# Reordering the mixer of a gated-attention-and-mixer kernel: the low-rank update a chunk ahead, the last chunk's second product kept for the next batch boundary, GpSimd transfers in written order

## The chip, the cores and the metric

The kernel runs on one core of a Trainium2 chip. The metric is the device time of one execution, in microseconds (us). Before the change it is 1245.14 us, the median of three runs (1243.36 to 1246.68). In this text PE is the matrix engine (PEld its weight loads), DVE the vector engine, ACT the scalar engine, POOL is GpSimd, and SP is the engine that issues the transposing transfers and the stores.

## The reference, cut to what matters

```python
# 8 batches; u, v: (8, 3136, 256); z: (8, 3136, 64); all float32
scores = (1.0 / S) * np.matmul(z, z.transpose(0, 2, 1))
x = u * np.matmul(np.maximum(scores, 0.0) ** 2, v)          # gated attention
xt = x.transpose(0, 2, 1)                                   # then the mixer
h = xt @ U @ V                                              # U: (3136, 32), V: (32, 3136)
u2 = x + h.transpose(0, 2, 1)
out = u2 + np.maximum(u2 @ w_ch1, 0.0) @ w_ch2              # 256 -> 1024 -> 256
```

## The kernel before

Each batch has 25 tiles of 128 rows. Attention handles one tile per turn (25 matmuls of 256 columns, 2.73 us). The scores are symmetric, so the kernel computes half of them and gets the other half by transposing DMAs ("strip"). When a pair of tiles is done, DVE multiplies it by u into `x_bf`, and SP transposes it into `uT`. When all 25 tiles are done comes the batch boundary: the rank product `x^T U` (t1), then the mixer, in seven chunks of three or four tiles. For every chunk there is

- a **mix**: two matmuls give V^T t1 for the chunk, and DVE adds them into `uT` in place;
- four **up** steps: `uT` times w_ch1, and ACT applies the relu;
- a **down** step for each tile: relu times w_ch2 (with one matmul more for the tile's V^T t1), and a DVE output add when a tile or a pair of tiles is done.

```python
ps2_pool = ctx.enter_context(tc.tile_pool(name="ps2", bufs=2, space=bass.MemoryType.PSUM))
# mm() chains every matmul to the one before, so PE runs in the order written.

def mix_steps(b, c):
    ...                                   # two matmuls into a ps2 buffer, then:
    dst = uT[:, :, c0 : c0 + w]
    dve(nc.vector.tensor_tensor(out=dst, in0=ps[:, :, :w], in1=dst, op=ALU.add), wait=False)

def mixer_steps(b, cs):
    steps = mix_steps(b, cs[0]) + up_steps(b, cs[0])
    for n, c in enumerate(cs):
        nxt = cs[n + 1] if n + 1 < len(cs) else None
        up = mix_steps(b, nxt) + up_steps(b, nxt) if nxt is not None else []
        down = down_steps(b, c)
        k = 0
        for i, s in enumerate(up):
            steps.append(s)
            while k < (i + 1) * len(down) // len(up):
                steps.append(down[k]); k += 1
        steps.extend(down[k:])
    return steps

# in each batch: chunks 3 to 6 of the batch before are spread into attention ("late")
    late = mixer_steps(b - 1, list(range(EARLY, NC))) if b else []
    ...
# at the boundary (cut): scores of the next batch, rank product, casts of v, then
    _spread(nxt[0], []); _spread(rank_steps(b), [])
    ...                                   # cast_v(0), cast_v(1), load_v
    _spread(nxt[1], [])
    early = mixer_steps(b, list(range(EARLY)))      # chunks 0 to 2
    early[0]()                                      # mix of chunk 0
    for s in rest[:3]: s()                          # two score steps and a strip
    for k, s in enumerate(early[1:]): s(); ...      # further score steps in between
```

Scores, mixes and up steps all draw on `ps2`, which has two buffers. A buffer comes free when ACT (scores, up) or DVE (mix) has read it. From chunk 1 on, a mix stands directly ahead of the first up step of its chunk.

## Time and profile before

| | before |
|---|---|
| time, median | 1245.14 us |
| PE busy / weight loads | 91% / 69% |
| ACT / DVE busy | 44% / 40% |
| chain of waits | PE 83%; the DVE add into uT is next |
| holes of PE, per boundary-to-boundary period | 11.7 to 15.0 us |
| holes of PE in the last mixer | 12.9 us |

"Holes" are my own sum over the timeline of matmuls. A hole is the start-to-start time of two matmuls beyond what the first takes back to back (109 ns for 256 columns, 176 for 416, 216 for 512). A period runs from 5 us ahead of one rank product to 5 us ahead of the next. Measured so, holes are real lost slots, while a busy share of PE is not: the Trainium skill, "Perfetto Trace Analysis", section "Identifying the Most-Contended Engine", says that matmul occupancy misjudges a pipelined PE and that weight-load occupancy is better. Here the page shows 91% for matmuls and 69% for weight loads, and the gaps decide.

The page of the profile, before: busy time of each engine, and the clock that PE was granted in 40 slices (tenths).

```profile
PE 1130.8 (91%) x8808; PEld 852.6 (69%) x8808; DVE 491.6 (40%) x773; ACT 542.5 (44%) x627; POOL 109.7 (9%) x194
PEclk8699999999999999999999998999999999999999
```

The list of waits before, for weight loads (engine, what ended the wait: us in total, times, longest).

```profile
PEld L81 <- issue: 83.5, 178, 2.1
PEld L81 <- DVE uT L361: 58.0, 34, 2.8
PEld L81 <- DVE zT L155: 16.4, 1, 16.4
```

The chain of waits before, by line.

```profile
by line: DVE uT L361 3.8%; ACT relu L388 1.8%; issue 1.2%; DMA zP<-z_bf 1.2%; DMA strip<-A_102 0.8%; DVE v_bf L176 0.8%; DMA v_raw<-in_v_dram 0.6%; SPq L247 0.6%; DMA strip<-A_91 0.6%; DMA z_raw<-in_z_dram 0.5%; PE ps_348 L81 0.5%; PE ps_11
```

The timeline of PE before, at the second boundary (start, duration, what it computes, count; in brackets the idle time ahead of it and what ended it).

```profile
300.20 0.59 PE L81 MATMUL ps_2909<-V_bf,t_sb 128*128 128x512 bf16 x2 [0.60 <-ACT A_103 L237]
300.95 0.51 PE L81 MATMUL ps_2913<-zT 128*128 128x416 bf16 x2 [0.16 <-ACT A_103 L237]
302.11 0.51 PE L81 MATMUL ps_2918<-zT 128*128 128x416 bf16 x2 [0.64 <-DVE uT L361]
...
308.76 0.59 PE L81 MATMUL ps_2960<-V_bf,t_sb 128*128 128x512 bf16 x2 [0.40 <-ACT relu L388]
310.67 1.04 PE L81 MATMUL ps_2965<-uT,w_bf 128*128 128x512 bf16 x4 [1.32 <-DVE uT L361]
...
318.76 0.59 PE L81 MATMUL ps_3051<-V_bf,t_sb 128*128 128x512 bf16 x2
321.71 1.04 PE L81 MATMUL ps_3056<-uT,w_bf 128*128 128x512 bf16 x4 [2.35 <-DVE uT L361]
```

A mix is `V_bf,t_sb`, an up step is `uT,w_bf`. Each up step that directly follows its mix waits for the DVE add, for 1.3 and 2.35 us here. The add itself takes 1.22 us; the rest of the longer wait is a 0.95 us cast of v that DVE had in front.

### The profile page before, as it was taken

The page shows a single profiled execution, that of the slowest core. Times are in us where ns is not written, and L with a number is a line of the kernel's source. Part 1 is how long each engine was busy: PE and PEld are TensorE (multiplying, and loading weights), DVE is VectorE, ACT ScalarE, POOL GpSimd, SP SyncE. Part 2 cuts the span into 40 slices and gives each one's busy share as a digit, 9 for nine tenths or more (in the row PEclk, how much of TensorE's full clock was granted, in tenths as well). Part 3 has the DMA queues.
Part 4 walks back from the last instruction along what each step waited for, and adds up shares of the span by engine and source line. Part 5 has one row for each costly group of instructions (what it writes and reads, how often), then busy time and mean ns, then how long its engine had stood idle before and what let it go on. Part 6 is the DMA issues. An engine that isn't in the chain of part 4 may idle for free.

```text
span 1242.8 us, 21094 instructions
## 1 busy us (share of the span) xinstructions
PE 1130.8 (91%) x8808; PEld 852.6 (69%) x8808; DVE 491.6 (40%) x773; ACT 542.5 (44%) x627; POOL 109.7 (9%) x194
## 2 busy tenths in 40 slices
PE   2698989998899988999799998999889998899987
PEld 1277757785678856788477874778657885678845
DVE  4742534335343353424434253443543334332122
ACT  3441555436452464425645255542635346451043
POOL 2500100000000000010000000000000010000000
PEclk8699999999999999999999998999999999999999
DMA  8589846785558956598565865778746795267811
GB/s 196 121 179 180 172 135 158 155 175 149 147 129 179 167 125 145 128 190 150 134 153 136 190 149 126 156 157 170 164 123 140 168 175 135 77 135 153 159 36 71
DMA packets 418288, 182.93 MB, mean 147 GB/s; under 512 B 389728, under 2 KB 395664, under 8 KB 418192
## 3 DMA queue, kind: packets, MB, share of 16 engines
q1 hardware_dynamic: 402112, 121.71, 49.4%
q0 software_dynamic: 16080, 59.87, 17.5%
q8 instruction: 69, 1.13, 0.4%
q14 instruction: 27, 0.22, 0.1%
HBM read 61.91 MB, written 25.69 MB: 70 GB/s over the span
## 4 chain that ended last, share of the span: by engine, by line
PE 83%; DVE 7%; DMA 4%; ACT 4%; issue 1%; SPq 1%; DVEq 0%; ACTq 0%
DVE uT L361 4%; ACT relu L388 2%; DMA zP<-z_bf 1%; DMA strip<-A_102 1%; DVE v_bf L176 1%; DMA v_raw<-in_v_dram 1%; SPq L247 1%; DMA strip<-A_91 1%; DMA z_raw<-in_z_dram 1%; PE ps_348 L81 0%; PE ps_11941 L81 0%; PE ps_10502 L81 0%; PE ps_9471 L81 0%; PE ps_8957 L81 0%; PE ps_8637 L81 0%
## 5 line engine op out<-in xcount | busy, mean ns | idle before, releaser
L81 PEld LDWEIGHTS <-strip 128*128 128x128 bf16 x2400 | 235.6, 98 | 60.5 <-DMA strip<-A_102 6.1
L81 PEld LDWEIGHTS <-relu 128*128 128x128 bf16 x1600 | 160.2, 100 | 29.7 <-issue 2.5
L81 PEld LDWEIGHTS <-w_bf 128*128 128x128 bf16 x896 | 86.5, 100 | 121.7 <-DVE uT L361 58.0
L81 PEld LDWEIGHTS <-zT 128*128 128x128 bf16 x800 | 79.5, 100 | 82.7 <-issue 49.7
L265 POOL DMA_DIRECT2D u_sb<-in_u_dram x96 | 52.8, 550 | 707.4 <-DVE x_bf L292 701.1
L176 DVE CAST v_bf<-v_raw 128x1536 bf16<-128x1536 f32 x32 | 30.5, 953 | 3.0 <-DMA v_raw<-in_v_dram 3.0
L168 POOL DMA_DIRECT2D v_raw<-in_v_dram x32 | 18.8, 587 | 118.4 <-DVE zT L155 34.7
L81 PEld LDWEIGHTS <-V_bf 128*128 128x128 bf16 x200 | 20.0, 100 | 10.8 <-issue 2.4
L329 ACT CAST t_sb<-ps_11997 128x256 bf16<-128x256 f32 x1 | 0.4, 372 | 46.3 <-PE ps_11997 L81 46.3
L81 PEld LDWEIGHTS <-t_sb 128*128 128x128 bf16 x112 | 10.8, 97 | 13.8 <-issue 10.0
L238 DVE TENSOR_TENSOR A_106<-A_106 128x832 bf16<-128x832 bf16 x16 | 9.5, 591 | 25.5 <-ACT A_106 L237 25.5
L238 DVE TENSOR_TENSOR A_101<-A_101 128x832 bf16<-128x832 bf16 x16 | 12.2, 763 | 12.3 <-ACT A_101 L237 12.3
L238 DVE TENSOR_TENSOR A_110<-A_110 128x832 bf16<-128x832 bf16 x16 | 9.5, 593 | 18.2 <-ACT A_110 L237 18.2
L238 DVE TENSOR_TENSOR A_97<-A_97 128x832 bf16<-128x832 bf16 x16 | 10.4, 651 | 15.2 <-ACT A_97 L237 15.2
L238 DVE TENSOR_TENSOR A_108<-A_108 128x832 bf16<-128x832 bf16 x16 | 9.5, 592 | 17.0 <-ACT A_108 L237 17.0
L81 PE MATMUL ps_156<-zT 128*128 128x416 bf16 x2 | 0.9, 528 | 16.8 <-DVE zT L155 16.8
L238 DVE TENSOR_TENSOR A_109<-A_109 128x832 bf16<-128x832 bf16 x16 | 9.5, 593 | 16.1 <-ACT A_109 L237 16.1
L155 DVE COPY zT<-zP 64x1536 bf16<-64x1536 bf16 (+3 forms) x20 | 12.8, 642 | 7.6 <-DMA zP<-z_bf 7.1
L238 DVE TENSOR_TENSOR A_98<-A_98 128x832 bf16<-128x832 bf16 x16 | 9.4, 591 | 15.8 <-ACT A_98 L237 15.8
L238 DVE TENSOR_TENSOR A_112<-A_112 128x832 bf16<-128x832 bf16 x16 | 9.5, 592 | 15.5 <-ACT A_112 L237 15.5
L238 DVE TENSOR_TENSOR A_95<-A_95 128x832 bf16<-128x832 bf16 x16 | 9.4, 590 | 15.0 <-ACT A_95 L237 15.0
L238 DVE TENSOR_TENSOR A_111<-A_111 128x832 bf16<-128x832 bf16 x16 | 9.5, 593 | 14.6 <-ACT A_111 L237 14.6
(3457 smaller groups left out, 2984.6 us busy)
## 6 DMA issues: line engine op xcount, KB each, us to landing
v_raw<-in_v_dram POOLq DMA_DIRECT2D x32, 768.0 KB, 5.7
u_sb<-in_u_dram POOLq DMA_DIRECT2D x96, 256.0 KB, 3.7
out_dram<-o_sb SPq DMA_DIRECT2D x80, 256.0 KB, 2.3
z_raw<-in_z_dram POOLq DMA_DIRECT2D x7, 768.0 KB, 4.8
out_dram<-o_sb SPq DMA_DIRECT2D x32, 128.0 KB, 2.3
uT<-x_bf SPq DMA_TRANSPOSE x200, 3.5
v_tmp<-in_moe_V_dram POOLq DMA_DIRECT2D x8, 192.0 KB, 4.5
w_bf<-in_moe_w_ch_dram POOLq DMA_DIRECT2D x2, 512.0 KB, 8.9
```

The costliest lines, as they stand in the source:

```text
L81: ins = nc.tensor.matmul(**kw)
L155: nc.vector.tensor_copy(out=zT[:dqk, t0 + h : e : 2, :], in_=zP[h * dqk : (h + 1) * dqk, t0 // 2 : _ceil_div(e, 2), :],)
L168: nc.gpsimd.dma_start(out=v_raw, in_=rows(v[b])[:, k * n_v : (k + 1) * n_v, :])
L176: dve(nc.vector.tensor_copy(out=v_bf[:, k * n_v : (k + 1) * n_v, :], in_=v_raw))
L238: nc.vector.tensor_tensor(out=dst, in0=dst, in1=dst, op=ALU.mult)
L247: nc.sync.dma_start_transpose(out=strip, in_=slot(b, o)[:, P:])
L265: nc.gpsimd.dma_start(out=u_sb[:, :nq, :], in_=rows(u[b])[:, o : o + nq, :])
L329: nc.scalar.copy(out=t1_sb, in_=ps[:, :D])
L361: nc.vector.tensor_tensor(out=dst, in0=ps[:, :, :w], in1=dst, op=ALU.add),
L388: nc.scalar.activation(out=relu[:, hp : hp + 2, :w], in_=ps[:, :, :w], func=AF.Relu)
```

## The change

The change has three intents. Every mix is to be issued a chunk ahead of its up steps, so that the add is hidden. The last chunk's down steps are to be kept for the next boundary, where they fill the time of the score steps, of the t1 copy and of the first add. GpSimd's transfers are to be issued in written order instead of the scheduler's. Keeping the chunk needs four spare x tiles in odd batches, since the next batch's x would overwrite tiles 8 to 11. The steps are also merged more evenly, and the chunk sizes move from 4,4,4,4,3,3,3 to 4,4,4,3,3,3,4.

```diff
+    def pool_dma(**kw):                  # every GpSimd transfer chained to the one before
+        ins = nc.gpsimd.dma_start(**kw)
+        ...
-    x_bf = persist.tile([P, NT, D], BF16, name="x_bf")
+    x_bf = persist.tile([P, NT + SPARE, D], BF16, name="x_bf")      # SPARE = 4
...
+    def merge(*lists):                   # even interleaving by relative position
...
+    def mixer_steps(b, cs, down=()):
+        steps = []
         for n, c in enumerate(cs):
-            ...
+            steps += merge(up_steps(b, c), mix_steps(b, cs[n + 1]) if 0 < n < len(cs) - 1 else [], down)
+            down = down_steps(b, c)
...
-        late = mixer_steps(b - 1, list(range(EARLY, NC))) if b else []
+        if b:
+            cs = list(range(EARLY, NC))
+            late = mixer_steps(b - 1, cs, down_steps(b - 1, EARLY - 1))
+            left = down_steps(b - 1, NC - 1)
...
-            fill = fill + late[done:upto]
+            fill = merge(fill, late[done:upto])
             if more and i == NT - 8:             # as before, but now in this order on the queue
                 load_v(b + 1, 0)
                 load_v(b + 1, 1)
...
+        seq = merge(ahead[:2], left[:2]) + rank_steps(b) + merge(ahead[2:4], left[2:3])
+        seq += mix_steps(b, cs[0]) + left[3:] + ahead[4:5] + mix_steps(b, cs[1])
...
+            early = merge(early, vs, ahead[5:])
+            early += mix_steps(b, EARLY) + mix_steps(b, EARLY + 1)
```

More of the change, by code (lines that the diff above doesn't have):

```diff
@@ L89, in mm @@
         last[0] = ins.ins.name
+    last_pool = [None]
+    def pool_dma(**kw):
+        ins = nc.gpsimd.dma_start(**kw)
+        if last_pool[0] is not None:
+            tc.add_manual_dep(
+                ins.ins,
+                last_pool[0],
+                mybir.DependencyInfo(mybir.DependencyClass.NoSync, mybir.DependencyReason.DATA),
+                reason="pool order",
+            )
+        last_pool[0] = ins.ins.name
     last_dve = [None]
@@ L109 @@
     v_bf = persist.tile([P, NT, D], BF16, name="v_bf")
-    x_bf = persist.tile([P, NT, D], BF16, name="x_bf")
+    SPARE = 4
+    x_bf = persist.tile([P, NT + SPARE, D], BF16, name="x_bf")
     uT = persist.tile([P, ND, S], BF16, name="uT")
@@ L120, in col, with home @@
         return (t - FIRST) * P if t >= FIRST else S - FIRST * P + t * P
+    def home(b, t):
+        return NT + t - (FIRST - SPARE) if b % 2 and FIRST - SPARE <= t < FIRST else t
     def rows(ap):
@@ L126, with load_z @@
     z_tiles = {}
-    def load_z(b, parts, eng):
+    def load_z(b, parts, start):
         z_raw = stage.tile([P, NT, dqk], FP32, name="z_raw", tag="stage")
@@ L134, in load_z @@
         for t0 in range(0, NF, n):
-            eng.dma_start(out=z_raw[:, t0 : t0 + n, :], in_=rows(z[b])[:, t0 : t0 + n, :])
-        eng.dma_start(out=z_raw[:TAIL, NF, :], in_=z[b, NF * P :, :])
+            start(out=z_raw[:, t0 : t0 + n, :], in_=rows(z[b])[:, t0 : t0 + n, :])
+        start(out=z_raw[:TAIL, NF, :], in_=z[b, NF * P :, :])
         for t0 in range(0, NF, n):
@@ L167, in load_v @@
         if k < 4:
-            nc.gpsimd.dma_start(out=v_raw, in_=rows(v[b])[:, k * n_v : (k + 1) * n_v, :])
+            pool_dma(out=v_raw, in_=rows(v[b])[:, k * n_v : (k + 1) * n_v, :])
         else:
-            nc.gpsimd.dma_start(out=v_raw[:TAIL, 0, :], in_=v[b, NF * P :, :])
+            pool_dma(out=v_raw[:TAIL, 0, :], in_=v[b, NF * P :, :])
         v_tiles[k] = v_raw
@@ L180, in load_weights @@
     def load_weights():
-        nc.gpsimd.dma_start(out=w1_bf, in_=moe_w_ch1.rearrange("(t p) d -> p t d", p=P))
-        nc.gpsimd.dma_start(out=w2_bf, in_=moe_w_ch2.rearrange("(t p) d -> p t d", p=P))
-        nc.gpsimd.dma_start(out=U_bf[:, :NF, :], in_=rows(moe_U))
-        nc.gpsimd.dma_start(out=U_bf[:TAIL, NF, :], in_=moe_U[NF * P :, :])
+        pool_dma(out=w1_bf, in_=moe_w_ch1.rearrange("(t p) d -> p t d", p=P))
+        pool_dma(out=w2_bf, in_=moe_w_ch2.rearrange("(t p) d -> p t d", p=P))
+        pool_dma(out=U_bf[:, :NF, :], in_=rows(moe_U))
+        pool_dma(out=U_bf[:TAIL, NF, :], in_=moe_U[NF * P :, :])
         for p0 in range(0, P, P // 2):
@@ L188, in load_weights @@
             for g in range(G):
-                nc.gpsimd.dma_start(
+                pool_dma(
                     out=v_tmp[g * R : (g + 1) * R, :, :],
@@ L204, in load_weights @@
         for g in range(G):
-            nc.gpsimd.dma_start(
+            pool_dma(
                 out=v_tmp[g * R : (g + 1) * R, :TAIL], in_=moe_V[:, NF * P :]
@@ L264, in begin @@
                 if o < NF:
-                    nc.gpsimd.dma_start(out=u_sb[:, :nq, :], in_=rows(u[b])[:, o : o + nq, :])
+                    pool_dma(out=u_sb[:, :nq, :], in_=rows(u[b])[:, o : o + nq, :])
                 else:
-                    nc.gpsimd.dma_start(out=u_sb[:TAIL, 0, :], in_=u[b, NF * P :, :])
+                    pool_dma(out=u_sb[:TAIL, 0, :], in_=u[b, NF * P :, :])
                 acc[0] = (ps, u_sb)
@@ L292, in end @@
                     nc.vector.tensor_tensor(
-                        out=x_bf[:p, t0 : t0 + nq, :],
+                        out=x_bf[:p, home(b, t0) : home(b, t0) + nq, :],
                         in0=ps[:p, : nq * D].rearrange("p (t d) -> p t d", d=D),
@@ L301, in end @@
                     nc.sync.dma_start_transpose(
-                        out=uT[:, :, col(t) : col(t) + P], in_=x_bf[:, t, :]
+                        out=uT[:, :, col(t) : col(t) + P], in_=x_bf[:, home(b, t), :]
                     )
@@ L323, in run @@
                     lhsT=U_bf[:, t, :],
-                    rhs=x_bf[:, t, :],
+                    rhs=x_bf[:, home(b, t), :],
                     start=(t < G),
@@ L338 @@
     chunks = []
-    for i, n in ((0, 4), (4, 4), (8, 4), (12, 4), (16, 3), (19, 3), (22, 3)):
+    for i, n in ((0, 4), (4, 4), (8, 4), (12, 3), (15, 3), (18, 3), (21, 4)):
         ts = [turns(i + k) for k in range(n)]
@@ L437, in step @@
                         in0=ps[:p, : nk * D].rearrange("p (t d) -> p t d", d=D),
-                        in1=x_bf[:p, ta : ta + nk, :],
+                        in1=x_bf[:p, home(b, ta) : home(b, ta) + nk, :],
                         op=ALU.add,
@@ L456, in flat @@
         return [s for part in lists for s in part]
-    def mixer_steps(b, cs):
-        steps = mix_steps(b, cs[0]) + up_steps(b, cs[0])
+    def merge(*lists):
+        keyed = [
+            ((i + 0.5) / len(part), n, s)
+            for n, part in enumerate(lists)
+            for i, s in enumerate(part)
+        ]
+        return [s for _, _, s in sorted(keyed, key=lambda e: e[:2])]
+    def mixer_steps(b, cs, down=()):
+        steps = []
         for n, c in enumerate(cs):
-            nxt = cs[n + 1] if n + 1 < len(cs) else None
-            up = mix_steps(b, nxt) + up_steps(b, nxt) if nxt is not None else []
+            steps += merge(up_steps(b, c), mix_steps(b, cs[n + 1]) if 0 < n < len(cs) - 1 else [], down)
             down = down_steps(b, c)
-            k = 0
-            for i, s in enumerate(up):
-                steps.append(s)
-                while k < (i + 1) * len(down) // len(up):
-                    steps.append(down[k])
-                    k += 1
-            steps.extend(down[k:])
         return steps
     nc.vector.memset(zT[dqk:, :, :], 0.0)
-    load_z(0, 3, nc.sync)
+    load_z(0, 3, nc.sync.dma_start)
     place_z(0, 3)
@@ L491 @@
         more = b + 1 < B
-        late = mixer_steps(b - 1, list(range(EARLY, NC))) if b else []
+        late, left = [], []
+        if b:
+            cs = list(range(EARLY, NC))
+            late = mixer_steps(b - 1, cs, down_steps(b - 1, EARLY - 1))
+            left = down_steps(b - 1, NC - 1)
         done = 0
@@ L502 @@
             upto = min(len(late), (i + 1) * len(late) // (FIRST - 1))
-            fill = fill + late[done:upto]
+            fill = merge(fill, late[done:upto])
             done = upto
             if more and i == 2:
-                load_z(b + 1, 1, nc.gpsimd)
+                load_z(b + 1, 1, pool_dma)
             if more and LEAD + i == NT:
@@ L515 @@
         k = FIRST - 1
-        nxt = [score_steps(b + 1, j) if more else [] for j in range(k, LEAD)]
-        for n, steps in enumerate(nxt[1:]):
-            if more:
-                steps.append(lambda n=n: turn(b + 1, FIRST + n))
-        _spread(nxt[0], [])
-        _spread(rank_steps(b), [])
+        ahead = []
+        if more:
+            for j in range(k, LEAD):
+                ahead += score_steps(b + 1, j)
+                if j >= FIRST:
+                    s = ahead.pop()
+                    ahead.append(lambda s=s, j=j: (s(), turn(b + 1, j)))
+        cs = list(range(EARLY)) if more else list(range(NC))
+        seq = merge(ahead[:2], left[:2]) + rank_steps(b) + merge(ahead[2:4], left[2:3])
+        seq += mix_steps(b, cs[0]) + left[3:] + ahead[4:5] + mix_steps(b, cs[1])
+        for s in seq:
+            s()
+        early = mixer_steps(b, cs)
         if more:
@@ L525, with late_v @@
                 load_v(b + 1, k + 2)
-        _spread(nxt[1], [])
-        if more:
-            early = mixer_steps(b, list(range(EARLY)))
-            rest = flat(nxt[2:])
-            early[0]()
-            for s in rest[:3]:
-                s()
             n = len(early) // 4
-            for k, s in enumerate(early[1:]):
-                s()
-                if k == n:
-                    cast_v(2)
+            def late_v(k):
+                cast_v(k)
+                if k == 2:
                     load_v(b + 1, 4)
-                if k == 2 * n:
-                    cast_v(3)
-                if k == 3 * n:
-                    cast_v(4)
-                if k % 2 == 1 and 3 + k // 2 < len(rest):
-                    rest[3 + k // 2]()
-            for s in rest[3 + len(early[1:]) // 2 :]:
-                s()
-        else:
-            for s in mixer_steps(b, list(range(NC))):
-                s()
+            vs = [lambda k=k: late_v(k) for k in (2, 3, 4)]
+            early = merge(early, vs, ahead[5:])
+            early += mix_steps(b, EARLY) + mix_steps(b, EARLY + 1)
+        else:
+            early += down_steps(b, NC - 1)
+        for s in early:
+            s()
 _INS = ['u', 'v', 'z', 'moe_U', 'moe_V', 'moe_w_ch1', 'moe_w_ch2']
```

## The prediction

> **What bounds the kernel.** TensorE. The page gives PE 91% of 1242.8 us; ACT has 44%, DVE 40%. The chain of waits is 83% PE; next come DVE's mix add into uT (3.8%) and ACT's relu (1.8%). The matmuls (8808) do not change, so only the holes in PE count. I read them off the timeline: start-to-start time beyond the back-to-back spacing (109 ns for 256 columns, 176 for 416, 216 for 512). About 38 us lie before the first boundary (loads, start-up scores, strip waits), which the change hardly touches. Each of the seven boundary-to-boundary periods has 11.7 to 15.0 us (97 us in all), the last mixer 12.9.
>
> One period (from 293 us): four score steps in a row around the rank product, 1.5 us together (ACT takes 0.86 us for one, PE 0.35, and ps2 has two buffers); the t1 copy 0.8; first u^T add 1.1; score and up steps that wait for ACT 2.1; second add 1.48; third 2.52; two more inside attention, 1.28 and 0.67. An add takes 1.22 us (1024 wide) or 0.95 (768), and its first product follows the mix at once. In the last mixer seven adds cost 1.2 to 1.65 each, t1 and the rank's wait 1.3.
>
> The Trainium skill, "TensorE: Matmul & The Clock Gate", section "What's actually happening", says that PE's clock is gated by how busy PE was. The trace agrees: 3.4 us windows at half clock, one or two, follow the holes at six of seven boundaries; each costs up to 1.7 us.
>
> **What the change does.** Each mix is issued a chunk before its up steps, so adds run behind 3 us or more of matmuls. The last chunk's four down steps (0.98 us each) are kept for the boundary: they separate the score steps and cover the t1 copy and first add. It adds no work that counts. GpSimd's written order puts v ahead of the weights at the start; v loads land 5.7 us after issue.
>
> **What remains per boundary (hand estimate from those durations).** The adds now stand in DVE's order among casts of v (0.95 us each). Second mix waits for the first add, ~0.2; first up steps wait for ps2 and ACT (1.02 against 0.86), 1.5 to 2.5; third add behind the cast that waits for the third v load, 0 to 2; usual small holes 1.5 to 2. So about 5 us instead of 13.9: 8.5 saved per boundary, but 5 at the first, which has no kept chunk. 6 x 8.5 + 5 = 56 us, and about 9 in the last mixer: 65. I take off 4 for new waits.
>
> **Prediction: 1184 us**, 8 in 10 between 1168 and 1206. Faster by over 2%: 0.95; within 2%: 0.04; slower: 0.01.
>
> **What shows it right.** PE near 95% busy; weight loads' waits for DVE uT (58 us in the list of waits) under 15; that line under 1% of the chain; periods of about 139 us; few half-clock windows between 170 us and the end; the last mixer about 55 us instead of 65; start-up (first boundary at 150 us) within 3 us.
>
> **What would make it wrong.** DVE, in order, stuck behind a v or z cast whose load is late, holding an add and so a ps2 buffer; boundary up steps still ACT-bound; a u load behind a v load that waits for a cast; V_bf casts on GpSimd falling onto the start of attention; strips (4.5 us) late because score steps now run to the boundary's end.

## The result, and the profile after

The changed kernel takes 1177.61 us (median of four runs, 1173.25 to 1180.37) beside 1245.91 us for the kernel before in the same rounds. The ratio is 0.9449, 95% interval 0.9413 to 0.9485. All ratios here are the mean time of one kernel's fast runs over that of the kernel before's fast runs of the same rounds, so they are not quite the ratios of the quoted medians. A second call gave 1174.95 us and 0.9438 (0.9412 to 0.9465).

The same lines of the page, after:

```profile
PE 1107.4 (95%) x8808; PEld 847.7 (72%) x8808; DVE 492.8 (42%) x765; ACT 546.8 (47%) x627; POOL 107.0 (9%) x194
PEclk7698999999999999999999999999999999999999
```

The list of waits after, for weight loads; the uT add is gone from it.

```profile
PEld L81 <- issue: 64.1, 128, 3.6
PEld L81 <- DMA strip<-A_92: 9.0, 1, 9.0
PEld L81 <- DVE zT L175: 8.7, 1, 8.7
```

The chain of waits after, by line: the add fell from 3.8% to 1.6%, and DMAs into strips stand at the head.

```profile
by line: DMA strip<-A_109 2.1%; DVE uT L381 1.6%; ACT relu L408 1.4%; DMA strip<-A_92 1.4%; DMA strip<-A_95 1.2%; issue 1.2%; DMA strip<-A_97 1.1%; DMA strip<-A_105 0.7%; SPq L321 0.5%; PE ps_912 L81 0.5%; PE ps_5735 L81 0.5%; PE ps_4270 L8
```

The timeline of PE after, at the same boundary.

```profile
288.89 0.59 PE L81 MATMUL ps_2887<-V_bf,t_sb 128*128 128x512 bf16 x2
289.32 0.27 PE L81 MATMUL ps_2870<-t_sb,V_bf 128*128 128x256 bf16 x1
289.43 1.04 PE L81 MATMUL ps_2870<-w_bf,relu 128*128 128x256 bf16 x8
290.31 0.52 PE L81 MATMUL ps_2903<-zT 128*128 128x416 bf16 x2
290.80 0.59 PE L81 MATMUL ps_2908<-V_bf,t_sb 128*128 128x512 bf16 x2
291.77 1.02 PE L81 MATMUL ps_2919<-uT,w_bf 128*128 128x512 bf16 x4 [0.38 <-ACT A_104 L257]
293.54 1.02 PE L81 MATMUL ps_2925<-uT,w_bf 128*128 128x512 bf16 x4 [0.74 <-DVE uT L381]
294.40 0.52 PE L81 MATMUL ps_2931<-zT 128*128 128x416 bf16 x2
295.67 1.02 PE L81 MATMUL ps_2938<-uT,w_bf 128*128 128x512 bf16 x4 [0.76 <-ACT relu L408]
```

Between the mix at 288.89 and its up step at 291.77 stand a kept down step, a score step and the next mix, so the add costs nothing. What is left are up steps that wait for a ps2 buffer (ACT, or the second add). Summed over the profile (us of holes; the start includes the time ahead of the first matmul):

```
                                    before   after
start, to the first boundary          55.2    53.7
seven periods (sum)                   97.0    36.6
last mixer                            12.9     2.7
all                                  165.1    93.0
```

The difference, 72.1 us, agrees within 1 us with that of the two spans (1242.8 and 1171.5, so 71.3). Half-clock windows of 3.4 us, which before followed the holes at six of seven boundaries, follow none of them after.

The start hides two larger moves. The first matmul comes at 9.0 us instead of 16.8, because v, and not the weights, now stands first on GpSimd's queue: its first load starts at 11.7 us, so that no GpSimd load runs beside those of z (before, the weights started at 1.7 us), and the third cast of z starts at 5.2 us instead of 7.9. But in batch 0, PE then stands still for 8.6 us at 104 us, which the list of waits after shows for matmuls:

```profile
PE ps_912 L81 <- DMA strip<-A_92: 8.6, 1, 8.6
PE ps_191 L81 <- DVE A_92 L253: 3.4, 1, 3.4
PE ps_288 L81 <- DVE A_102 L253: 2.6, 1, 2.6
PE ps_8657 L81 <- DMA strip<-A_109: 1.7, 1, 1.7
```

So the first rank product begins at 148.7 us instead of 150.2. Later batches also have strip waits (0.6 to 1.9 us, in four of seven periods) that the kernel before had nowhere after batch 0.

### The profile page after: what moved, and what is told of

The parts are those of the page before. It is cut to its first block, busy times and chain, and to the rows that moved or that the text cites. A ratio compares the mean times of both kernels' runs of the same rounds, so it can differ in the third digit from the quotient of the medians.

```text
span 1171.5 us, 21059 instructions
## 1 busy us (share of the span) xinstructions
PE 1107.4 (95%) x8808; PEld 847.7 (72%) x8808; DVE 492.8 (42%) x765; ACT 546.8 (47%) x627; POOL 107.0 (9%) x194
## 4 chain that ended last, share of the span: by engine, by line
PE 84%; DMA 8%; DVE 3%; ACT 2%; issue 1%; SPq 1%; DVEq 0%; POOLq 0%
DMA strip<-A_109 2%; DVE uT L381 2%; ACT relu L408 1%; DMA strip<-A_92 1%; DMA strip<-A_95 1%; DMA strip<-A_97 1%; DMA strip<-A_105 1%; SPq L321 1%; PE ps_912 L81 0%; PE ps_5735 L81 0%; PE ps_4270 L81 0%; PE ps_8134 L81 0%; PE ps_9557 L81 0%; PE ps_9423 L81 0%; PE ps_8016 L81 0%
## 5 line engine op out<-in xcount | busy, mean ns | idle before, releaser
L81 PEld LDWEIGHTS <-relu 128*128 128x128 bf16 x1600 | 156.5, 98 | 28.4 <-ACT relu L408 0.6
L95 POOL DMA_DIRECT2D u_sb<-in_u_dram x104 | 56.5, 543 | 710.2 <-DVE x_bf L312 702.7
L95 POOL DMA_DIRECT2D v_raw<-in_v_dram x40 | 22.5, 565 | 215.6 <-DVE v_bf L196 204.4
L258 DVE TENSOR_TENSOR A_104<-A_104 128x832 bf16<-128x832 bf16 x16 | 12.2, 765 | 22.8 <-ACT A_104 L257 22.8
L258 DVE TENSOR_TENSOR A_100<-A_100 128x832 bf16<-128x832 bf16 x16 | 10.7, 671 | 18.2 <-ACT A_100 L257 18.2
L258 DVE TENSOR_TENSOR A_96<-A_96 128x832 bf16<-128x832 bf16 x16 | 9.3, 588 | 19.9 <-ACT A_96 L257 19.9
L258 DVE TENSOR_TENSOR A_108<-A_108 128x832 bf16<-128x832 bf16 x16 | 9.5, 592 | 19.5 <-ACT A_108 L257 19.5
L258 DVE TENSOR_TENSOR A_101<-A_101 128x832 bf16<-128x832 bf16 x16 | 11.3, 708 | 14.8 <-ACT A_101 L257 14.8
L258 DVE TENSOR_TENSOR A_109<-A_109 128x832 bf16<-128x832 bf16 x16 | 9.5, 591 | 18.8 <-ACT A_109 L257 18.8
L258 DVE TENSOR_TENSOR A_106<-A_106 128x832 bf16<-128x832 bf16 x16 | 9.4, 590 | 19.0 <-ACT A_106 L257 19.0
L258 DVE TENSOR_TENSOR A_107<-A_107 128x832 bf16<-128x832 bf16 x16 | 9.5, 591 | 18.6 <-ACT A_107 L257 18.6
L258 DVE TENSOR_TENSOR A_111<-A_111 128x832 bf16<-128x832 bf16 x16 | 9.5, 592 | 18.5 <-ACT A_111 L257 18.5
L258 DVE TENSOR_TENSOR A_110<-A_110 128x832 bf16<-128x832 bf16 x16 | 9.5, 591 | 18.0 <-ACT A_110 L257 18.0
L258 DVE TENSOR_TENSOR A_113<-A_113 128x832 bf16<-128x832 bf16 x16 | 9.5, 591 | 17.7 <-ACT A_113 L257 17.6
L258 DVE TENSOR_TENSOR A_93<-A_93 128x832 bf16<-128x832 bf16 x16 | 9.4, 591 | 17.7 <-ACT A_93 L257 17.7
L258 DVE TENSOR_TENSOR A_95<-A_95 128x832 bf16<-128x832 bf16 x16 | 9.4, 589 | 17.3 <-ACT A_95 L257 17.3
```

The lines of the kernel that those rows point to most:

```text
L81: ins = nc.tensor.matmul(**kw)
L95: ins = nc.gpsimd.dma_start(**kw)
L258: nc.vector.tensor_tensor(out=dst, in0=dst, in1=dst, op=ALU.mult)
```

## The experiments

Theory A was that matmul order (the mix ahead, the kept chunk) is the gain. Rivals were that the transfers' written order is much of it (C), and that one of the two matmul parts is nearly all of it (B). Twelve kernels ran; all gave correct outputs.

### The transfers' order alone, taken away and added

```diff
 e1_pool_free (on the kernel after)
-        if last_pool[0] is not None:
+        if False:
 e2_before_ordered (on the kernel before)
-        nc.gpsimd.dma_start(...)       everywhere
+        pool_dma(...)
```

> The kernel after, with the GpSimd transfers left to the scheduler's order (weights ahead of v at the start, v loads spread over attention as before). Theory A (the gain is matmul order; the transfers' written order is near neutral because it starts PE 8 us earlier and then loses 9 us to one wait for a strip in batch 0): 1170 to 1182 us, first matmul back at about 16.8 us, no strip wait over 6 us at 104 us. Rival C (the written order itself is worth much of the 68 us): over 1195 us.

> The kernel before, with the GpSimd transfers in written order and nothing else. Theory A: 1238 to 1252 us (within 1% of before); first matmul at about 9 us instead of 16.8, and a strip wait of 5 to 10 us later in batch 0 that takes it back. Rival C: under 1225 us.

Measured: e1 1169.39 us, ratio 0.9377 (0.9363 to 0.9392); e2 1255.29 us, ratio 1.0066 (1.0035 to 1.0097). Theory A's size was right within a few us, but "neutral" was wrong: the written order costs 0.6 to 0.7% both ways, about 8 us. Rival C falls. In e2 the first matmul indeed starts at 9.2 us and a 10.4 us wait for a strip follows at 104 us; five of its seven later periods have a strip wait of 0.9 to 2.5 us. In e1 there is none after batch 0, and its periods are 137.6 us, five times 138.4, and 130.0 (in the kernel after 137.6, then 138.4 to 140.3, and 130.0). The holes of e1 are not set beside those above: its trace lacks 47 of the 8808 matmul records (those of e2 to e11 lack 24 to 47), and a missing one counts as a hole of up to 0.2 us.

### One of the two matmul parts undone

```diff
 e3_not_kept (on the kernel after)
-            left = down_steps(b - 1, NC - 1)
+            late += down_steps(b - 1, NC - 1)
 e4_mix_at_its_up (on the kernel after)
-            steps += merge(up_steps(b, c), mix_steps(b, cs[n + 1]) if ... else [], down)
+            steps += merge(mix_steps(b, c) + up_steps(b, c), down)
-        seq += mix_steps(b, cs[0]) + left[3:] + ahead[4:5] + mix_steps(b, cs[1])
+        seq += left[3:] + ahead[4:5]
-            early += mix_steps(b, EARLY) + mix_steps(b, EARLY + 1)
```

> The kernel after, but the last chunk's down steps stay in the attention stage (nothing kept for the boundary). Theory A: the score steps around the rank product, the t1 copy and the first u^T add lose their cover, about 3 to 3.5 us of holes per boundary at six boundaries: 1192 to 1202 us, some half-clock windows back. Rival (kept chunk is worth nothing, the mix order is all): 1174 to 1182 us.

> The kernel after, but each mix directly ahead of its own chunk's up steps, as before; the kept chunk, chunk sizes and written order stay. Theory A: the adds' holes return, 5 to 7 us per period and 8 to 9 us in the last mixer: 1215 to 1235 us, with half-clock windows at most boundaries. Rival B (the spreading of ACT's work by the kept chunk is the main part): under 1200 us.

Measured: e3 1186.81 us, ratio 0.9536 (0.9486 to 0.9586), between the two expectations: the kept chunk is worth 9 to 12 us (against the kernel after), not the 14 to 27 that theory A's 1192 to 1202 us meant. e4 1208.84 us, ratio 0.9691 (0.9675 to 0.9708), less than theory A expected. Undoing both one at a time explains 40 to 46 us of some 79 (e2 to after), so the parts are not simply additive, or something else in the rewriting carries the rest.

e4 also turned out to be no clean edit. The first mix moved behind the casts of v in the program, so DVE does both casts ahead of the add. The timeline of DVE and PE in e4, at a boundary:

```profile
438.12 0.95 DVE L196 CAST v_bf<-v_raw 128x1536 bf16<-128x1536 f32 x1
438.98 0.58 DVE L258 TENSOR_TENSOR A<-A 128x832 bf16<-128x832 bf16 x1
439.48 0.95 DVE L196 CAST v_bf<-v_raw 128x1536 bf16<-128x1536 f32 x1
440.35 1.22 DVE L381 TENSOR_TENSOR uT<-ps,uT 128x1024 bf16<-128x1024 f32 x1
...
441.62 1.04 PE L81 MATMUL ps<-uT,w_bf 128*128 128x512 bf16 x4 [4.00 <-DVE uT L381]
```

This one wait, 4.0 us at each of six boundaries, makes 24 of the 31 to 34 us that e4 costs. So e4 says little about the other mixes, which here have a down step behind them. In its list of waits for weight loads:

```profile
PEld L81 <- DVE uT L381: 25.7, 6, 4.3
```

### Both undone, and the neighbour of a mix fixed

```diff
 e9_neither = the edits of e3 and e4 together
 e10_glued (on e4: the mix and its first up step become one step)
-            steps += merge(mix_steps(b, c) + up_steps(b, c), down)
+            (mix,), up = mix_steps(b, c), up_steps(b, c)
+            up[0] = lambda mix=mix, u0=up[0]: (mix(), u0())
+            steps += merge(up, down)
```

> The kernel after with both main parts undone: each mix directly ahead of its own up steps, and nothing kept for the boundary; even merging, chunk sizes and written order stay. If mix order and kept chunk cover the same holes (undoing one alone cost 11 and 33 us, 44 of about 76): 1240 to 1258 us, as the kernel before in written order (1255). If instead the even merging by itself does part of the work (it lets a down step fall between a mix and its first up step): 1215 to 1235 us.

> As the run with each mix at its own up steps and the kept chunk, but with the mix and the first up step glued together, so that the merging can put no down step between them, as it was in the kernel before. If that down step is why undoing the mix order cost only 33 us where 39 to 59 were expected: the uncovered adds (1.2 to 1.6 us, 3 more per period and 5 in the last mixer) come back, 1230 to 1245 us. If not: 1206 to 1212 us.

Measured: e9 1201.95 us, ratio 0.9635 (0.9602 to 0.9668); e10 1306.53 us, ratio 1.0477 (1.0444 to 1.051). Both lie outside what was written, and they tell the most. With neither a mix ahead nor a kept chunk, the kernel is still 53 us faster than the kernel before in written order. The even merging lets one down step (0.98 us) fall between a mix and its up step. The timeline of PE in e9, in the last mixer:

```profile
1151.66 0.59 PE L81 MATMUL ps<-V_bf,t_sb 128*128 128x512 bf16 x2
1152.09 0.27 PE L81 MATMUL ps<-t_sb,V_bf 128*128 128x256 bf16 x1
1152.20 1.04 PE L81 MATMUL ps<-w_bf,relu 128*128 128x256 bf16 x8
1153.57 1.02 PE L81 MATMUL ps<-uT,w_bf 128*128 128x512 bf16 x4 [0.33 <-DVE uT L381]
```

and in e10, where nothing may stand in between, in the early and in the late part of one mixer:

```profile
480.56 0.59 PE L81 MATMUL ps<-V_bf,t_sb 128*128 128x512 bf16 x2
482.63 1.04 PE L81 MATMUL ps<-uT,w_bf 128*128 128x512 bf16 x4 [1.49 <-DVE uT L381]
...
492.50 0.43 PE L81 MATMUL ps<-V_bf,t_sb 128*128 128x320 bf16 x2
495.41 0.72 PE L81 MATMUL ps<-uT,w_bf 128*128 128x320 bf16 x4 [2.48 <-DVE uT L381]
```

The list of waits of weight loads in e10, in e9 and, for comparison, in e2:

```profile
PEld L81 <- DVE uT L381: 131.0, 54, 9.8
```

```profile
PEld L81 <- DVE uT L381: 10.9, 6, 1.8
```

```profile
PEld L81 <- DVE uT L374: 59.7, 34, 3.0
```

e10 is slower than the kernel before, and slower than I expected. The kernel before had a mix and its up step as two steps in the late chunks, and attention's matmuls fell between them; the glue forbids that too. So e10 exposes an add for nearly every chunk (54 waits, 56 chunks), and many half-clock windows follow. It shows the cost of a bare add; it is not a copy of the kernel before.

From e2 by e9 and e3 to the kernel after, each a step nearer to it, the ratios (each against the kernel before in its own rounds) are 1.0066, 0.9635, 0.9536, 0.9438. That is 4.3% of the time before for the even merging with the rest of the rewriting (chunk sizes, the spread of score steps), 1.0% for issuing the mix a chunk ahead, 1.0% for the kept chunk. The intervals of e3 and of the kernel after all but touch, the sizes depend on the order in which the parts are added, and the first step was not divided further by a run. The traces divide it. Summed from the first boundary on, by what ended them, the holes are (us, those over 20 ns):

```
                        before    e2    e9    e3  after
DVE add into uT           57.4  59.0  16.0  16.2    7.9
ACT (scores and relu)     25.6  27.4  23.1  24.3   15.0
```

- The first step took away 43 us of waits for the add, of its 53 in all. So most of it is cover for the adds. That the even merging alone gives it, without the other rewriting, no run shows.
- Issuing the mix a chunk ahead left these waits as they were (16.0 and 16.2 us); they only moved. e9's profile has eight half-clock windows in this stretch and e3's has one. At up to 1.7 us each, that could be the 1.0%; it was not tested.
- The kept chunk took away 17.6 us, close to the 3 us per boundary of theory A, yet the times differ by 9 to 12 us. e3's profile is of its slowest run (1198.9 us) and has more strip waits than the kernel after, so the rest stays open.

### Loads of v against strips

The two v loads are written at turn 17 of 25. The queue runs ahead of PE, so they are issued late in turn 13 (turns are counted from 0). In turns 9 to 13 attention has no score steps between its matmuls, and from turn 11 on no steps of the mixer either, so it needs a strip every 2.73 us. In the trace after, the loads of batch 0 start at 96.6 and 97.1 us and land after 8.9 and 10.5 us. The strip issued at 96.8 us lands after 16.0 us, the next after 10.9. The Trainium skill, "DMA: Bandwidth & Descriptors", section "Issuing engines are not separate DMA queues", says that transfers of all issuers run on the same 16 DMA engines and interleave; that fits. The next runs move the loads.

```diff
 e5_v_apart (on the kernel after): the two loads written at turns 19 and 23
 e11_v_early (on the kernel after): the two loads written at turns 6 and 11
 e8_start_ordered (on the kernel after)
-        if last_pool[0] is not None:
+        if last_pool[0] is not None and starting[0]:      # off once the weights are issued
```

> The kernel after, with the first two v loads of the next batch at turns 19 and 23 of 25 instead of both at turn 17. Theory V (the 9 us wait for a strip in batch 0 and the 0.6 to 1.9 us ones later come from two 768 KB loads back to back on the DMA engines that the strip transposes need): strip waits after 95 us under 2 us in all, 1160 to 1170 us. Rival T (the SP queue of transposes itself is too slow where attention has no other steps in between): the 9 us wait stays within 3 us, 1172 to 1181 us.

> The kernel after, all in written order, with the first two v loads of the next batch written at turns 6 and 11 instead of both at 17, which puts them on the queue near turns 3 and 9. Theory V: 1159 to 1167 us, strip waits after batch 0 all under 0.5 us. If written order itself is the evil (u loads waiting behind v loads), it stays at 1173 to 1181 us.

> The kernel after, with the GpSimd transfers in written order only up to the weights (v ahead of the weights) and left to the scheduler from then on (v loads early in attention, as in the run with the free order). Theory V (loads of v in the stretch of attention that has no other steps, turns 9 to 13, starve the strip transposes): keeps the early start (first matmul at 9 us) and has no strip wait over 4 us: first rank product at 140 to 144 us, 1160 to 1166 us, with little scatter. Rival (the early start is worth nothing because the strips of batch 0 are bound by their own queue): as the free order, 1167 to 1171 us.

Measured: e5 is unsteady. Its three fast runs (within 1.5% of its fastest) are 1163.3, 1165.9 and 1176.2 us (ratio 0.9376, 0.9339 to 0.9412), the other three 1180.8 to 1208.8, over 1.5% above the fastest. Its profile fell in a slow run, so I take no size from it, and whether moving the loads later helps is not shown. e11: 1162.07 us, ratio 0.9334 (0.9305 to 0.9362). e8: 1160.16 us (1158.41 to 1161.89), ratio 0.9309 (0.9284 to 0.9333). Both early placements hit. The rank product of batch 0 begins at 141.1 us in e11 and 140.4 in e8, instead of 148.7: the early start is kept. After batch 0 neither has a strip wait of 0.5 us or more. Written order as such is not the fault, since e11 keeps it; where it puts the v loads is.

Why these places are good is not shown. After batch 0, e8 and e11 issue one load in turns 1 to 3 and the other at turn 9.0, where the stretch without other steps begins; in the kernel after both come at its end. And e5's edit issues them one at a time in turns 15 and 19, outside it; yet in the profile of e7, a fast run that has this edit too, strips still took up to 23.3 us. So theory V's stretch of turns 9 to 13 does not explain it, and two loads back to back is not the whole cause either.

Strip transfers at 96 to 114 us in the kernel after and in e8 (the last line of each: time to landing).

```profile
who waited for it (us, times):
  PEld L81: 10.3, 2
  PE ps_912 L81: 8.6, 1
...
DMA to landing us min/median/max: 3.7/8.0/16.0
```

```profile
who waited for it (us, times):
  DVE x_bf L313: 2.0, 1
...
DMA to landing us min/median/max: 3.8/4.9/6.9
```

### The holes that are left at a boundary

```diff
 e6_up_before_mix (on the kernel after)
-        seq += mix_steps(b, cs[0]) + left[3:] + ahead[4:5] + mix_steps(b, cs[1])
+        seq += mix_steps(b, cs[0]) + left[3:]
+        # then: two up steps, mix of chunk 1, casts of v, two up steps;
+        # score steps from the fifth on are spread behind them
 e7_both = e5 and e6
```

> The kernel after, unchanged, as the mark for the three runs beside it: 1173 to 1181 us.

> The kernel after, with the second mix of a boundary behind two of the first chunk's up steps and no score step among those up steps. Theory: the holes left at a boundary (0.54, 0.90, 0.92, 0.41 us: ps2 buffers that wait for ACT and for the second u^T add) fall from 2.8 to 1.2 to 1.8 us per boundary; 7 to 11 us in all: 1165 to 1171 us. Rival (ACT's total work in this stretch is what binds, so the order cannot help): within 3 us of the kernel after.

> Both of the edits beside it. If they are independent, the savings add: 1152 to 1162 us. If not, no better than the better of the two.

Measured: the mark 1174.95 us (its interval is above; one run of 1184.4 lies above what was expected); e6 1181.57 us, ratio 0.9495 (0.9472 to 0.9519); e7 1188.69 us, ratio 0.952 (0.9479 to 0.9561). The edit failed: e6 is slower than the mark. In e6 the holes of the first 38 us of a boundary are 4.3 to 4.7 us at most boundaries, against 4.0 in the mark's profile (both traces lack 47 matmul records). That is too little for the 6.6 us between the two medians; the rest is open. The first waits became smaller and new ones for ACT appeared, among them one of 0.74 us (idle, by the timeline) behind the third mix. That agrees with the rival, that ACT's total work there binds, but no run here changed ACT's work, so it is not shown. e7 is no better than e6 (the intervals overlap), and I leave that open: its profile has an 8.3 us strip wait in batch 2.

## Why the prediction was right

The prediction was 1184 us, 1168 to 1206; measured, 1177.61 and 1174.95.

- **Holes per boundary.** 13.9 us were to become about 5; they became 5.2 (36.6 over seven). Saved in the seven periods: 60 us, with 56 predicted; the first boundary saved 7.4 us and not 5.
- **Last mixer.** About 9 us were to go; 10.2 went. Its length from the rank product is 57.2 us, not "about 55", from 64.8.
- **What remains.** Second mix 0.2 us: measured 0.15. Up steps 1.5 to 2.5: measured 2.8 (0.54, 0.90, 0.92, 0.41). Third add behind a late v load 0 to 2: measured 0.
- **Clock.** Few half-clock windows after 170 us: there was none until the last microseconds. Six periods lie at 137.6 to 140.3 us, as forecast; the last one, in which no scores of a next batch are computed, takes 130.0 (140.1 before).
- **PE and chain.** PE was to be near 95% busy, and is. The weight loads' waits for the uT add were to fall from 58.0 to under 15 us; their list names none after. The add was to be under 1% of the chain; it is 1.6%, through the up step that waits for the second mix's buffer.
- **New waits.** Four us were taken off. The run with the free order shows about 8 us of cost. The forecast saving, 61 us, was 11 below the 72.1 us of holes saved: 4.4 of it in the periods, 1.2 in the last mixer, 1.5 at the start, and the 4 taken off, since the periods are already counted with their new strip waits. The start within 3 us came out (1.5 us), but as the sum of 7.8 us gained and most of it given back at a strip, which I had not foreseen. I had listed v loads only as blocking u loads, and not as slowing the strips.
- **Whose gain.** The prediction gave the saving to "each mix is issued a chunk before its up steps" and to the kept chunk. The mechanism, matmuls between a mix and its up steps, holds. But the whole chunk of distance is not what pays: with the mix at its own up steps and nothing kept, the evenly merged kernel, with one down step in between, already has most of it (1255 to 1202 us, and 43 us less waiting for the add).

## What to carry to other kernels

If a matrix step reads what another engine has just rewritten, put about as much other matrix work between them as that engine needs. Here about one microsecond of cover came with most of the gain, and the larger reordering added little. Fixing an order on a transfer queue fixes where large loads meet small urgent ones. Test that part alone, and try more than one place for the loads: here the order cost 8 us inside a gain of 70, and two other placements gave the fastest kernels, 1160 and 1162 us.

## What the Trainium skill lacked or had wrong

- "TensorE: Matmul & The Clock Gate" ("What's actually happening", and the table "Why this matters for your kernels") ties the half clock to an idle window of about 3.4 us and advises against idle gaps over about 3 us. A further section, "A second HAM failure mode: psum-queue depth-cycling", says that frequent micro-idles of PE between groups of matmuls make the clock swing too, but not how much idle it takes. Here no hole at a boundary exceeds 2.52 us, and the clock still halves: the nine windows ahead of a drop, from the first boundary on in the kernel before, have PE busy 31 to 48% of the time. It is no sharp limit, for one window at 43% (173.8 to 177.2 us) was not followed by a drop. Three of the nine (window, its length, busy time and count of each engine, clock, DMA):

```profile
453.66:457.08 3.42, 1.53 (x6) 0.50 (x6) 1.71 (x3) 1.79 (x3) 0.00 (x0) 1.00 0.46 104
467.32:470.73 3.41, 1.35 (x9) 0.84 (x10) 2.00 (x2) 0.22 (x1) 0.20 (x1) 1.00 0.78 179
614.09:617.50 3.41, 1.06 (x7) 0.32 (x5) 2.69 (x3) 0.25 (x1) 0.20 (x1) 1.00 0.81 192
```

- "DMA: Bandwidth & Descriptors" says that all issuers share the 16 engines, but has no figure for a transposing transfer beside large loads. Here a strip, which takes 3.6 to 6.6 us in nine of ten cases in the kernel after, took 16.0 us beside two loads of 768 KB.
